# Seven products instead of eight in three more sets of a tile's up stage, and its attention steps at set slots

## The chip, the cores and the metric

The kernel runs on one core of one Trainium2 chip. The core has a matrix engine (PE, with its weight loader PEld), a vector engine (DVE), a scalar engine (ACT), a general engine (POOL) and a queue engine (SP) that only issues transfers; each works through its own instructions in order and waits on semaphores for the others. The metric is the device time of one execution in microseconds. Three runs of the kernel before took 1019.09, 1018.75 and 1016.43 us, so their median is 1018.75 us. The execution that was profiled took 1014.55 us.

## The reference

```python
# q, k, v: (8, 8, 576, 64), float32
scores = scale * np.matmul(q, k.transpose(0, 1, 3, 2))
gamma = 1.0 - 2.0 ** (-5.0 - np.arange(H, dtype=np.float32))
Dmat = np.where(rel >= 0, gamma[:, None, None] ** rel[None, :, :], 0.0)
ret = scores * Dmat[None, :, :, :]
attn_out = np.matmul(ret, v)
# (B, H, S, D) -> x: (4608, 512)
g = x @ w_gate                      # 512 -> 1536
silu = g * (1.0 / (1.0 + np.exp(-g)))
val = x @ w_val
return silu * val @ w_out           # 1536 -> 512
```

A retention attention without softmax gives 4608 tokens of 512 features; a gated feed-forward block follows. All is float32.

## The kernel before, in words

**Tiles and stages.** The tokens are worked in five tiles: tile 0 has 512 tokens, tiles 1 to 4 have 1024 each. What the change calls tile two is the second of them, `n == 1` in the code. Each of the big tiles has an up stage (`up_stage`, both projections and the gating) and a down stage (`down_step`, 26 steps, the output projection). The attention of the tokens that the next tile needs runs in between as attention steps (`tick`): there is one for each batch and pair of heads, and it is put between two pieces of the stages' work.

**The up stage.** The 1536 hidden columns are taken in three thirds (`qd` 0, 1, 2). For each third the product of the tile with the weights is made by a two-level scheme of the Strassen-Winograd kind. The outer level turns it into seven sets, worked in the order `SETS = (1, 2, 6, 7, 4, 5, 3)`. Each set is itself a product of two by two blocks, and is made either plainly, by eight products (`whole_slot`), or again by seven (`slot`). `PLAIN` lists the sets of tile two that are made plainly. One product is one slot: two matmuls of 128x128 weights with 128x256 activations, one for the gate and one for the value (`multiply`, L1186). A plain set is eight slots, filling four PSUM banks one after the other, two slots each; a seven-product set has five slots of its own (products 1, 5, 2, 6, 3) and leaves its products 7 and 4 to be put between the slots of the set that follows.

**Who reads the banks.** For a plain set, DVE adds each full bank to what the other sets left (`whole_read`, `combine` at L1042): one read for each of the four corners, two in set 5. For a seven-product set the bank is read while the sum in it grows: products 6, 7 and 4 are accumulated into the bank of product 1, product 3 into that of product 5, and each further product may be written only when the reading before it is done (`first_read`, `second_read`). That is seven reads for most sets. Corner results of sets 2, 4, 5 and 3 lie in four buffers (`ends`, one for each corner in tile two); `finish` takes them from there: ACT makes the SiLU (L1200) and DVE or POOL the product with the value part (L1201; in tile two DVE, but POOL for set 2 and in the last third). `clear` sees to it that a corner's buffer is finished before another set writes to it.

**Sums of operands.** The seven-product form needs sums of the blocks of the weights and of the tile. In tile two POOL makes the weights' sums during the stage itself (`w_outer`, `w_inner`, L1042), since SP also stores them for the later tiles (L1119 to L1122); they go through three block buffers in turn. The sums of a set of the tile's own blocks are made by `x_inner` (four sums of 128x256), and it overwrites one block of the set in place. The dictionary `after` holds at which slot each of these is issued; within an engine the order of issue is the order of work, and no engine waits for a slot as such.

**An attention step.** `tick` puts the matmuls of a step on PE at once and leaves the rest as pieces: ACT copies a state and the outputs to the next tile (L584, L656, L626), DVE masks the scores (L580, L590), makes the states (L596, L603, L608) and transposes the next queries and keys (L492, `qT` and `kT`); SP issues the loads of a later step (L282, L287). In the up stage a piece is taken at every second slot, and what is left is issued when the next step comes (`go_on(len(pieces))` at the head of `tick`). The scores of a step (L573) read the `kT` that the pieces of the step before it transposed.

**Where the steps stand.** In tile two's up stage of 157 slots, `merge` spreads six steps evenly over the slots from 56 on: they come ahead of slots 56, 73, 90, 106, 123 and 140, and the first of them has no matmuls. Four steps stand in the down stage, ahead of down steps 2, 7, 13 and 19:

```python
cut = (done + upto + (n == 1) * 2) // 2
merge((0.0, ticks(done, cut)), (0.5, ups))
for i, f in reversed(list(zip((2, 7, 13, 19), ticks(cut, upto), strict=True))):
    downs.insert(i, f)
```

The weights' operands of the down stage come through a ring of eight buffers (`fetch_one`), the first five over ACT's queue and the later ones over SP's.

Of the kernel before, what the change touches and what calls it, by code (L numbers as in the profile page):

```python
# [106 lines left out]


SETS = (1, 2, 6, 7, 4, 5, 3)
PLAIN = {(1, qd, o) for qd in range(3) for o in (1, 2, 4, 5, 3) if qd == 0 and o == 1 or o in (4, 5, 3)}  # L110


def terms(text):
# [18 lines left out]
def kernel(  # L132
# [45 lines left out]
    TW = 1024  # L178
    TB = TW // 4
    NF = DF // P  # L180
    NQ = NF // 4
# [32 lines left out]
    w_up = arena[:, QW : 4 * QW].rearrange("p (q g h k x) -> p q g h k x", q=NQ, g=2, h=4, k=2)  # L214
# [8 lines left out]
    xs = {0: rest[:, x0_at:dn_at].rearrange("p (h t) -> p h t", h=HP)}  # L223
    for n in range(1, NTILE):
        xs[n] = x_odd if n % 2 else rest[:, 0:QW].rearrange("p (h t) -> p h t", h=HP)
    at = [4096 + 512 * i for i in range(4)] + [x0_at + 512 * i for i in range(4)]
# [682 lines left out]
    for old, new in swaps.items():  # L909
        at = [i for i, line in enumerate(signed) if old in line]  # L910
# [136 lines left out]
    def x_sets(n):  # L1047

        x = xs[n].rearrange("p (K k) (T t x) -> p T K k t x", k=2, T=2, t=2)
        block = lambda a: rest[:, a : a + 1024].rearrange("p (k t x) -> p k t x", k=2, t=2)  # L1050
        sets = {1: x[:, 0, 0], 2: x[:, 0, 1], 4: x[:, 1, 1], 7: x[:, 1, 0], 5: block(4096), 6: block(5120), 3: block(x0_at)}
        spots = [rest[:, x0_at + 1024 + TB * i : x0_at + 1024 + TB * (i + 1)] for i in range(4)]
        spots += [rest[:, sum_at + 1024 + TB * i : sum_at + 1024 + TB * (i + 1)] for i in range(2)]
        spots += [rest[:, dn_at + 4096 + TB * i : dn_at + 4096 + TB * (i + 1)] for i in range(12)]
        spots += [operands[:, 5376 + TB * i : 5376 + TB * (i + 1)] for i in range(3)]
        new = {o: spots[3 * m : 3 * m + 3] for m, o in enumerate((4, 5, 1, 2, 6, 7, 3) if n == 1 else (1, 2, 7, 4, 5, 3, 6))}
        aside = new[3][2] if n > 1 else sets[1][:, 0, 1]

        def outer_sums(o, eng):
            a, b, sign = {5: (7, 4, 1), 6: (5, 1, -1), 7: (1, 7, -1), 3: (2, 6, -1)}[o]  # L1060
            return [lambda k=k: combine(eng, sets[o][:, k], sets[a][:, k], sets[b][:, k], sign) for k in range(2)]

        def inner_sums(o, eng):
            a, (s1, s2, s4) = sets[o], new[o]
            return [lambda: combine(eng, s1, a[:, 0, 1], a[:, 1, 1], 1),
                    lambda: combine(eng, s2, s1, a[:, 0, 0], -1),
                    lambda: combine(eng, aside if o == 1 else a[:, 0, 1], a[:, 0, 0], a[:, 0, 1], -1),
                    lambda: combine(eng, s4, a[:, 1, 0], s2, -1)]

        def put_back(eng):  # L1070
            a = sets[1]
            return [lambda: combine(eng, a[:, 0, 1], a[:, 0, 0], a[:, 0, 1], -1)]

        def view(o, i, qd):
            a, (s1, s2, s4) = sets[o], new[o]
            return {1: a[:, 0, 0], 2: a[:, 1, 0], 3: s4, 4: a[:, 1, 1], 5: s1, 6: s2, 7: aside if o == 1 and qd == 0 else a[:, 0, 1]}[i]

        return outer_sums, inner_sums, put_back, view, sets
# [55 lines left out]
    def up_stage(n):  # L1134

        busy, base = n == 1, used[0]
        x_outer, x_inner, put_back, x_at, x_raw = x_sets(n)
        seq = [(qd, o) for qd in range(NQ) for o in SETS]
        K = len(seq)
        plain = [(n, *e) in PLAIN for e in seq]  # L1140
        final = {2: (0, 0), 3: (0, 1), 4: (1, 0), 5: (1, 1)}
# [150 lines left out]
        slots, begins = [], []  # L1292
# [12 lines left out]
        if not busy:  # L1305
            begin = lambda k: begins[k]
            if n + 1 < NTILE:
                for i, f in enumerate(x_inner(2, nc.gpsimd)):
                    later(i, f)
                for i, f in enumerate(x_outer(7, nc.vector)):  # L1310
                    later(8 + 2 * i, f)
            for k, o in enumerate((6, 7, 4, 5, 3)):
                for i, f in enumerate(x_inner(o, nc.gpsimd)):
                    later(begin(k + 1) - (n + 1 == NTILE) * 3 + i, f)
            later(begin(6), *put_back(nc.gpsimd))
        else:
            for o, at in {7: 6, 1: 22}.items():
                for i, f in enumerate(x_inner(o, nc.gpsimd)):
                    later(at + i, f)
            for qd in range(NQ):  # L1320
                at = begins[len(SETS) * qd]
                _, _, w_outer, w_inner, store = w_sets(qd)
                if qd:
                    outers, inners = {5: 4, 6: 6, 7: 12, 4: 18}, {2: 0, 6: 8, 7: 14, 4: 20, 5: 27, 3: 34}
                else:
                    outers, inners = {7: 0, 4: 14}, {7: 2, 4: 18, 1: 28, 5: 35, 3: 39}
                for o, start in outers.items():
                    for i, f in enumerate(w_outer(o)):
                        later(at + start + i, f)
                for o, start in inners.items():  # L1330
                    for j, f in enumerate(w_inner(o)):
                        later(at + start + j, f)
                    later(at + start + 3, *store(o, True))
                if qd + 1 < NQ:
                    *_, next_inner, next_store = w_sets(qd + 1)
                    for j, f in enumerate(next_inner(1)):
                        later(at + (42 if qd else 44) + j, f)
                    later(at + (45 if qd else 47), *next_store(1, True))
                for i, o in enumerate((1, 2, 3, 5, 6, 7, 4)):
                    for j, f in enumerate(store(o, False)):  # L1340
                        later(at + (1, 2, 4, 8, 10, 15, 25)[i] + j, f)

        def go(at):
            for f in after.pop(at, ()):
                f()
            while waiting and waiting[0][0] <= at:
                finish(*waiting.pop(0)[1:])
            s = slots[at]
            (whole_slot if len(s) == 3 else slot)(*s, at)
            after_tick()  # L1350
            if at % (2 if busy or at >= 7 * len(SETS) else 3) == 1 and (busy or at % (7 * len(SETS)) < 36):
                part_on()
            if busy and at - begins[2 * len(SETS)] in (36, 38, 40):
                fetch_one()
            if at + 1 == len(slots):
                while waiting:
                    finish(*waiting.pop(0)[1:])
                for t in sorted(after):
                    for f in after[t]:
                        f()  # L1360
                after.clear()
                rested[:] = [i for b in free for i in range(4) if b is banks[i]]
                assert len(rested) == 4 and not taken
                if busy:
                    fetch_one()
                    fetch_one()
# [52 lines left out]
    def merge(*lists):  # L1419
        merged = [((i + d) / len(l), j, f) for j, (d, l) in enumerate(lists) for i, f in enumerate(l)]  # L1420
        for _, _, f in sorted(merged, key=lambda e: e[:2]):
            f()
# [81 lines left out]
    done = FIRST  # L1504
# [5 lines left out]
    ticks = lambda a, b: [lambda t=t: spread_tick(t) for t in range(a, b)]  # L1510
    for n in range(1, NTILE):
        upto = needed(n + 1) if n + 1 < NTILE else done
        cut = (done + upto + (n == 1) * 2) // 2
        ups = up_stage(n)
        if n == 1:

            for i in range(8 * len(SETS)):
                ups.pop(0)()
                if i in (13, 30):
                    wait = nc.sync.nop()  # L1520
                    tc.add_manual_dep(wait.ins, stepped[-1].ins.name,
                                      mybir.DependencyInfo(mybir.DependencyClass.Sync, mybir.DependencyReason.DATA), reason="loads in turn")
                    load(FIRST + i // 30)
        downs = [lambda i=i: down_step(n, i) for i in range(N)]
        if n == 1:
            merge((0.0, ticks(done, cut)), (0.5, ups))
        else:

            for i, f in reversed(list(zip((4, 52, 68, 102), ticks(done, cut)))):
                ups.insert(i, f)  # L1530
            merge((0.5, ups))
        if n == 1:

            for i, f in reversed(list(zip((2, 7, 13, 19), ticks(cut, upto), strict=True))):
                downs.insert(i, f)
            merge((0.5, downs))
        else:
            merge((0.0, ticks(cut, upto)), (0.5, downs))
        done = upto
# [30 lines left out]
```

## Time and profile before

| | |
|---|---|
| median of three runs | 1018.75 us (1016.43 to 1019.09) |
| profiled execution | 1014.55 us, its span 1012.8 us |
| PE busy | 1000.9 us, 99% of the span |
| DVE, POOL, ACT busy | 710.9, 561.8, 286.7 us |
| granted clock of PE | 1.000 |
| tile two's up stage | 172.2 to 319.4 us |
| tile two's down stage | 319.4 to 389 us |

The span runs from the first to the last instruction, and 1.75 us of the profiled execution lie around it. PE's matmul rows overlap their followers, so their busy time says little; the distance from one start to the next says how fast PE goes. A float32 matmul shows as two rows, so one slot is four rows. Rows of DVE, ACT and POOL that follow at once also overlap a little: two DVE reads in a row take less than twice one.

### The profile page before, as it was taken

The page shows a single profiled execution, that of the slowest core. Times are in us where ns is not written, and L with a number is a line of the kernel's source. Part 1 is how long each engine was busy: PE and PEld are TensorE (multiplying, and loading weights), DVE is VectorE, ACT ScalarE, POOL GpSimd, SP SyncE. Part 2 cuts the span into 40 slices and gives each one's busy share as a digit, 9 for nine tenths or more (in the row PEclk, how much of TensorE's full clock was granted, in tenths as well). Part 3 has the DMA queues.
Part 4 walks back from the last instruction along what each step waited for, and adds up shares of the span by engine and source line. Part 5 has one row for each costly group of instructions (what it writes and reads, how often), then busy time and mean ns, then how long its engine had stood idle before and what let it go on. Part 6 is the DMA issues. An engine that isn't in the chain of part 4 may idle for free.

```text
span 1012.8 us, 21319 instructions
## 1 busy us (share of the span) xinstructions
PE 1000.9 (99%) x8336; PEld 825.5 (82%) x8336; DVE 710.9 (70%) x1206; ACT 286.7 (28%) x636; POOL 561.8 (55%) x589
## 2 busy tenths in 40 slices
PE   6999999999999999999999999999999999999998
PEld 5655555888888888888888888888888888888887
DVE  4488887677875766977777678866575767566645
ACT  4565522132423312133422202233220012232110
POOL 3400359979375228575564157746672586566514
PEclk9999999999999999999999999999999999999999
DMA  9999866967587787647677777434454554445553
GB/s 245 261 288 272 192 216 234 264 193 214 138 238 207 217 231 193 198 156 196 184 202 206 198 179 217 154 133 159 161 172 141 154 189 147 148 155 180 182 159 102
DMA packets 278892, 194.38 MB, mean 192 GB/s; under 512 B 212552, under 2 KB 246088, under 8 KB 278792
## 3 DMA queue, kind: packets, MB, share of 16 engines
q1 hardware_dynamic: 251464, 94.70, 36.7%
q10 hardware_dynamic: 26688, 97.92, 29.1%
q8 instruction: 66, 1.08, 0.5%
q0 software_dynamic: 640, 0.39, 0.2%
q14 instruction: 34, 0.28, 0.1%
HBM read 154.04 MB, written 38.93 MB: 191 GB/s over the span
## 4 chain that ended last, share of the span: by engine, by line
PE 94%; DVE 2%; DMA 1%; POOL 1%; SPq 0%; issue 0%; ACT 0%; DVEq 0%; ACTq 0%; POOLq 0%
PE bankB L1186 12%; PE bankC L1186 11%; PE bankA L1186 11%; PE bankE L1186 11%; PE bankB L1392 7%; PE bankC L1392 7%; PE bankE L1392 6%; PE bankA L1392 6%; PE outer L532 2%; PE bankE L853 2%; PE bankA L853 2%; PE outer L1186 2%; PE inner L1186 2%; PE bankB L853 2%; PE outer L559 2%; PE bankC L853 2%
## 5 line engine op out<-in xcount | busy, mean ns | idle before, releaser
L1042 POOL TENSOR_TENSOR rest<-rest 128x512 f32<-128x512 f32 (+1 forms) x139 | 148.0, 1076 | 159.9 <-DVE rest L1042 112.5
L1201 POOL TENSOR_TENSOR arena<-rest,io 128x256 f32<-128x256 f32 x168 | 123.9, 750 | 89.4 <-ACT io L1200 88.9
L1200 ACT ACTIVATE io<-rest 128x256 f32<-128x256 f32 x192 | 79.3, 417 | 200.0 <-DVE rest L1042 140.0
L1186 PE MATMUL bankB<-rest,arena 128*128 128x256 f32 x448 | 114.5, 380 | 0.0
L1042 DVE TENSOR_TENSOR rest<-bankB,rest 128x512 f32<-128x512 f32 x116 | 78.5, 685 | 40.5 <-PE bankB L1186 28.5
L1186 PE MATMUL bankC<-rest,arena 128*128 128x256 f32 x416 | 106.3, 380 | 0.0
L1186 PE MATMUL bankA<-rest,arena 128*128 128x256 f32 x412 | 104.8, 379 | 0.0
L1042 DVE TENSOR_TENSOR rest<-bankA,rest 128x512 f32<-128x512 f32 x111 | 75.2, 685 | 40.8 <-PE bankA L1186 19.3
L1042 DVE TENSOR_TENSOR rest<-bankC,rest 128x512 f32<-128x512 f32 x110 | 74.5, 683 | 38.0 <-PE bankC L1186 23.4
L1042 DVE TENSOR_TENSOR rest<-bankE,rest 128x512 f32<-128x512 f32 x106 | 71.7, 684 | 36.2 <-PE bankE L1186 17.6
L1186 PE MATMUL bankE<-rest,arena 128*128 128x256 f32 x372 | 94.9, 380 | 0.3 <-DVE rest L1042 0.3
L1186 PEld LDWEIGHTS bankB<-rest,arena 128*128 128x128 f32 x448 | 84.7, 190 | 11.9 <-DVE rest L1042 0.2
L1186 PEld LDWEIGHTS bankC<-rest,arena 128*128 128x128 f32 x416 | 78.5, 190 | 11.4 <-DVE rest L1042 0.8
L1186 PEld LDWEIGHTS bankA<-rest,arena 128*128 128x128 f32 x412 | 78.1, 190 | 10.9 <-DVE rest L1042 0.2
L1186 PEld LDWEIGHTS bankE<-rest,arena 128*128 128x128 f32 x372 | 70.3, 190 | 10.4 <-DVE rest L1042 0.8
L1042 POOL TENSOR_TENSOR arena<-arena 128x256 f32<-128x256 f32 (+1 forms) x76 | 70.3, 947 | 11.1 <-PE bankC L1186 9.0
L886 POOL TENSOR_TENSOR rest<-rest 128x512 f32<-128x512 f32 x21 | 28.5, 1377 | 72.1 <-DVE rest L407 58.5
L1392 PE MATMUL bankB<-arena 128*128 128x256 f32 x264 | 61.0, 381 | 0.0
L1392 PE MATMUL bankE<-arena 128*128 128x256 f32 x264 | 60.8, 380 | 0.0
L1392 PEld LDWEIGHTS bankE<-arena 128*128 128x128 f32 x264 | 50.0, 190 | 6.9
L1392 PEld LDWEIGHTS bankB<-arena 128*128 128x128 f32 x264 | 49.8, 190 | 6.9
L1392 PE MATMUL bankC<-arena 128*128 128x256 f32 x240 | 55.2, 379 | 0.0
(270 smaller groups left out, 1876.0 us busy)
## 6 DMA issues: line engine op xcount, KB each, us to landing
arena<-up ACTq DMA_DIRECT2D x63, 896.0 KB, 4.6
arena<-dn ACTq DMA_DIRECT2D x65, 384.0 KB, 3.1
arena<-dn SPq DMA_DIRECT2D x39, 384.0 KB, 3.1
out_dram<-rest SPq DMA_DIRECT2D x31, 256.0 KB, 3.4
qk<-in_q_dram SPq DMA_DIRECT2D x108, 72.0 KB, 3.1
qk<-in_k_dram SPq DMA_DIRECT2D x108, 72.0 KB, 3.4
dn<-rest SPq DMA_DIRECT2D x26, 256.0 KB, 2.8
up<-arena SPq DMA_DIRECT2D x13, 512.0 KB, 5.6
```

Of the source, the lines that this page charges most:

```text
L532: m = nc.tensor.matmul(value(i, hl, c), s["v"][rows, at], ret[rows, c % 2 if whole(i) else hl, c // 2], start=start, stop=start, skip_grou ...
L559: nc.tensor.matmul(xr[half[hl]] if c + 1 == NC else value(i, hl, c), state[half[hl], c, :], s["qT"][half[hl], ts(c, L)], start=False, stop ...
L853: nc.tensor.matmul(bank, w, xs[0][:, c, :], start=(c == 0), stop=(c == HP - 1))
L886: eng.tensor_tensor(out=dst, in0=srcs[0], in1=srcs[1], op=ALU.add if op[0] == "add" else ALU.subtract)
L1042: eng.tensor_tensor(out=out, in0=a, in1=b, op=ALU.add if sign > 0 else ALU.subtract)
L1186: m = nc.tensor.matmul(b[:, g * TB : (g + 1) * TB], w[:, g], x, start=(opens and g == 0), stop=True, skip_group_check=True)
L1200: nc.scalar.activation(out=s, in_=src[:, 0:TB], func=AF.Silu)
L1201: (nc.vector if busy and o != 2 and qd + 1 < NQ else nc.gpsimd).tensor_tensor(out=hid[:, qd, 2 * H + h, 2 * T + t], in0=src[:, TB : 2 * TB ...
L1392: nc.tensor.matmul(b[:, m * TB : (m + 1) * TB], lhs[:, qd, ts(m, P)], w[:, qd], start=(opens and qd == 0 and m == 0), stop=(qd == NQ - 1), ...
```

## The change: three sets fewer in `PLAIN`, and slots given for the steps

Sets 3 of the second third and 4 and 3 of the last third are taken out of `PLAIN`, and so made by seven products. The stage has 154 slots instead of 157. `x_inner` is issued for set 3 from slot 38 of the second third and for set 4 from slot 17 of the last third, eight sums of 128x256 on POOL; their results go to room in the weights' region and in the next tile's. The steps of tile two's up stage stand ahead of slots 56, 70, 84, 97 and 111, one step fewer than before; the down stage has five, ahead of down steps 1, 5, 10, 14 and 19. Two of the first fetches for the down stage are issued one and three slots later.

```diff
-PLAIN = {(1, qd, o) for qd in range(3) for o in (1, 2, 4, 5, 3) if qd == 0 and o == 1 or o in (4, 5, 3)}
+PLAIN = {(1, qd, o) for qd in range(3) for o in (1, 2, 4, 5, 3) if qd == 0 and o == 1 or o in (4, 5, 3)} - {(1, 1, 3), (1, 2, 4), (1, 2, 3)}
...
+        if n == 1:
+            new[4] = [w_up[:, NQ - 1, 0, h, k, :] for h, k in ((0, 0), (1, 0), (0, 1))]
+            new[3] = [xs[2][:, h, TW - TB :] for h in range(3)]
...
-            for o, at in {7: 6, 1: 22}.items():
+            second, third = begins[len(SETS)], begins[2 * len(SETS)]
+            for o, at in {7: 6, 1: 22, 3: second + 38, 4: third + 17}.items():
...
-            if busy and at - begins[2 * len(SETS)] in (36, 38, 40):
+            if busy and at - begins[2 * len(SETS)] in (36, 39, 43):
                 fetch_one()
...
-        cut = (done + upto + (n == 1) * 2) // 2
+        cut = done + 5 if n == 1 else (done + upto) // 2
...
-            merge((0.0, ticks(done, cut)), (0.5, ups))
+            places_of = [i - 8 * len(SETS) for i in (56, 70, 84, 97, 111)]
         else:
-
-            for i, f in reversed(list(zip((4, 52, 68, 102), ticks(done, cut)))):
-                ups.insert(i, f)
-            merge((0.5, ups))
+            places_of = (4, 52, 68, 102)
+        for i, f in reversed(list(zip(places_of, ticks(done, cut)))):
+            ups.insert(i, f)
+        merge((0.5, ups))
...
-            for i, f in reversed(list(zip((2, 7, 13, 19), ticks(cut, upto), strict=True))):
+            for i, f in reversed(list(zip((1, 5, 10, 14, 19), ticks(cut, upto), strict=True))):
```

## The prediction, made before the changed kernel ran

> **What bounds the kernel now.** I read the page's busy times first, then the busy times by stretches, PE's waits in the stage, PE's order of time, and last the other engines' order of time where PE was nearest to waiting.
>
> ```profile
> PE 1000.9 (99%) x8336; PEld 825.5 (82%) x8336; DVE 710.9 (70%) x1206; ACT 286.7 (28%) x636; POOL 561.8 (55%) x589
> ...
> 172.35:319.60 147.25, 147.06 (x1242) 128.62 (x1241) 108.12 (x192) 44.16 (x107) 110.25 (x138) 1.00 0.72 202
> 319.60:389.00 69.40, 69.40 (x822) 60.88 (x821) 42.79 (x72) 19.30 (x55) 25.75 (x16) 1.00 0.79 215
> ...
> PE bankB L1186 <- ACT rest L1231: 0.2, 1, 0.2
> ```
>
> The two stretches are tile two's up and down stage; after the length come PE, PEld, DVE, ACT and POOL. PE is never without work, DVE and POOL are busy three quarters of the up stage, and PE's only wait there is 0.2 us. So fewer matmuls shorten the kernel as long as no new wait appears. How fast PE goes is read from starts:
>
> ```profile
> 180.82 1.03 PE L1186 MATMUL bankC<-x_odd,arena 128*128 128x256 f32 x4
> 181.69 1.03 PE L1186 MATMUL bankA<-rest,arena 128*128 128x256 f32 x4
> ...
> 251.38 0.46 PE L532 MATMUL outer<-ret,v 64*64 64x64 f32 x16
> ...
> 253.63 1.13 PE L1186 MATMUL bankB<-rest,arena 128*128 128x256 f32 x4
> 254.60 1.89 PE L1186 MATMUL bankA<-rest,arena 128*128 128x256 f32 x8
> ```
>
> One product (four rows) takes 0.863 us from start to start, not 1.03. An attention step takes 253.63 - 251.38 = 2.25 us, and the product behind it 0.10 more. The next rows are the stretch where PE came nearest to waiting, first DVE, then ACT, then POOL:
>
> ```profile
> 256.01 0.68 DVE L580 TENSOR_TENSOR ret<-inner,near 128x512 f32<-128x512 f32 x1
> 256.61 0.21 DVE L590 TENSOR_TENSOR ret_last<-outer,last_near 128x64 f32<-128x64 f32 x1
> 257.07 1.28 DVE L1042 TENSOR_TENSOR rest<-bankA,rest 128x512 f32<-128x512 f32 x2
> ...
> 266.69 0.77 DVE L492 STREAM_TRANSPOSE kT<-qk 128x576 f32<-128x576 f32 x1
> ...
> 272.82 0.21 ACT L656 COPY rest<-outer 128x64 f32<-128x64 f32 x1 [0.57 <-DVE ret_last L590]
> 272.93 1.13 ACT L626 COPY rest<-outer 128x256 f32<-128x256 f32 x3
> 274.09 0.59 ACT L1231 COPY rest<-bankB 128x512 f32<-128x512 f32 x1
> ...
> 251.88 4.33 POOL L1042 TENSOR_TENSOR arena<-arena 128x256 f32<-128x256 f32 x5
> 265.21 7.23 POOL L1042 TENSOR_TENSOR arena<-arena 128x512 f32<-128x512 f32 x7 [9.01 <-PE bankC L1186]
> 280.32 0.73 POOL L1201 TENSOR_TENSOR arena<-rest,io 128x256 f32<-128x256 f32 x1 [7.89 <-ACT io L1200]
> ```
>
> What to see: when a step comes, ACT's four output copies wait for `ret_last` on DVE and take 272.82 to 274.06, 1.24 us, and whatever ACT owes PE waits behind them (a bank copy; PE went on at 274.72, some 0.4 us late over two places). And POOL has two holes, 9.0 and 7.9 us.
>
> **What goes.** Three sets lose one product each: 3 x 0.863 = **-2.59 us**. The 0.4 us at 274 go too, as no step stands there any more: **-0.40**.
>
> **The moved step.** Its 136 matmul rows cost 2.35 us in either stage: 0. Its other work goes along: about 4.2 us of DVE, its ACT copies, and on SP ten to thirteen loads (5 to 6 us of issue). In the down stage DVE was busy 42.8 of 69.4 us and has room; steps there stand 4 or 5 down steps apart instead of 5 or 6. SP's operands of the down stage queue behind the loads, but eight buffers of 2.59 us each are 20 us of cover, against some 6. Price 0, up to 2 where one of DVE's sums is late (a rival). The loads themselves are issued up to 3 us nearer to their use in the up stage, with 13 us left: 0. The later fetches have over 10 us to their first use: 0.
>
> **The eight sums on POOL.** 8 x 0.69 = 5.5 us, in the holes of 9.0 and 7.9 us. Set 3's come right before the first hole and are done before PE needs them; set 4's come ahead of that set's weights' sums. Price on PE 0; without the holes each would cost its 0.7.
>
> **Nine reads more.** Seven reads a set instead of four, 0.60 us apart when they follow at once (257.07 and its pair take 1.28 with an end of 0.68): 5.4 us of DVE, while the step that left gives 4.2 back. On average that is hidden. It isn't at one place, which costs twice.
>
> Place one, `kT` of the step ahead of slot 97. The step before stands ahead of slot 84, 13 slots away (16 before), and the pieces are spread at the same pace, so that `kT` is transposed just ahead of the next step. DVE has in between, by the order of instructions: 9 reads (5.4), 5 products of `finish` (1.9), the step's own work (0.61 + 0.13 + 0.77 + 0.95 + 0.39 + two transposes of 0.69 = 4.2), it starts 0.45 late behind ACT's copy L584, and waits twice by some 0.6 at the start for a bank and a SiLU behind the four copies: 13.2 us. PE's 13 slots and the 1.6 us from the head of a step to its scores give 12.9. So 0.3 us late. The five products may be slower than that:
>
> ```profile
> L1201 DVE TENSOR_TENSOR arena<-rest,io 128x256 f32<-128x256 f32 x15 | 9.5, 636 | 1.6 <-ACT io L1200 1.6
> ...
> L1201 DVE TENSOR_TENSOR arena<-rest,io 128x256 f32<-128x256 f32 x5 | 2.1, 416 | 0.2 <-issue 0.2
> ```
>
> The first row is 197 to 253 us, with POOL busy, the second 256.3 to 265, in POOL's hole: 0.22 us each. With set 3's sums and the later clock POOL fills this place until about 261, so 5 x 0.22 = 1.1 us more. **+1.2 us** of bounds 0 and 2.4 (a DVE instruction or two more or less).
>
> [...]
>
> Place two, product 3 of the same set (slot 101). It accumulates into the bank of product 5, which DVE must have read; that read writes corner 22's buffer, which still holds the plain set's last corner, and so `clear` puts that corner's `finish` ahead of it. From the end of the step: product 1 full 0.98, read 0.60, `ret` 0.61, `ret_last` 0.21, ACT's four copies 0.05 + 1.24, the SiLU 0.42, DVE's product 0.05 + 0.41, the read 0.69 + 0.05: 5.3 us. PE is there after four slots, 3.45. **+1.9 us**, and 0.3 for a collision with POOL: **+2.2**, bounds 0 (ACT makes the SiLU ahead of the copies) and 3.2. Before, set 3 was plain and used corner 22 last.
>
> Smaller: the product after (slot 103) 0.25, and the last set of the stage, where 6, 3, 7 follow and product 7 waits for a read of 0.69 within one slot, 0.35: **+0.6**, bounds 0 and 1.5.
>
> Sum: -2.59 - 0.40 + 1.2 + 2.2 + 0.6 = **+1.0 us**, so 1014.55 + 1.0 = 1015.6 us for an execution like the profiled one. That execution lies 4.2 us below the median of the runs shown, so against the median it is 1018.75 + 1.0 = **1019.8 us**. Some 0.3%, 3 us, is what a measurement of this kernel can tell from no change: this is none.
>
> **The rivals**, all against the median. (A) The full gain: DVE and ACT keep up and PE doesn't wait. 1018.75 - 3.0 = 1015.8 us. For it: PE waited nowhere for DVE in this stage, with 108 us busy of 147. Against it: 14.8 of 16.2 us busy between 253.7 and 269.9, and steps that stand closer. (B) Slower: POOL is late for set 4's weights. Its sums wait for the hole's release by set 3 of the second third, at about 265, and for `finish` of set 2; from there four of those (2.8), outer sums (4.9), inner sums of set 7, x of set 4, weights of set 4 (8.3) take some 16 us, to about 295; PE needs the first at slot 132, about 298 with the waits above. It decides once POOL loses more than 4 us to collisions; then each further us is PE's. With POOL 30% slower, 2.5 us: 1018.75 + 1.0 + 2.5 = 1022.3. Against it: POOL's two holes. (C) The fifth step in the down stage makes a sum of DVE late; before, PE used one at 352.9 that ended at 352.6. One instruction of `reads` and one transpose ahead of it, with the hop itself: 1.5 to 2 us, 1021.5. [...] (E) The change doesn't do what it says: the order of instructions shows three products fewer and five steps, so no chance.
>
> **Numbers.** The forecast, gain and new waits nearly equal (1017 to 1021.8): 0.60. A 0.15, B 0.09, C 0.13, D 0.03. Below 1015.7 lies half of A: faster 0.08. Above 1021.8 lie most of B and D, a third of C and little of the forecast: slower 0.16. Within: 0.76. The range goes from A, with the scatter of three runs, 1015.2, to just beyond B, 1022.8.
>
> **What would show it.** Tile two's up stage 2.4 us shorter for the step that left, and otherwise 0 to 1 us longer; 12 matmul rows of L1186 fewer; a wait of PE at L573 for `kT`, and one of about 2 us at L1186 for a DVE read behind an L1201 whose release is ACT's SiLU. The down stage 2.4 us longer. If PE's waits show neither, it is A; if they name POOL's L1042, B; if they are at L1392, C.

## The result, and the profile after

The changed kernel took 1026.37 us (median of 1025.76, 1026.38, 1026.36 and 1029.57); the kernel before took 1018.25 us on the same chip. The ratio is 1.0095, with a 95% interval of 1.0074 to 1.0115: slower by almost one per cent, and outside the range of the prediction. The execution that was profiled took 1025.76 us, 11.2 us more than the profiled one of before.

The busy times of the page, as far as PE, show that the part meant to go did go: twelve matmul rows fewer than before (8336).

```profile
PE 1002.4 (98%) x8324; PEld 824.3 (81%) x8324; DVE 724.5 (71%) x1216; ACT 286.4 (28%) x636; POOL 567.3 (55%) x597
```

Next come the busy times by stretches, for the changed kernel. The stretches are tile two's up stage, its down stage as far as down step 22, and from there to tile three; after the length stand PE, PEld, DVE, ACT and POOL, then the granted clock.

```profile
173.02:318.85 145.83, 142.66 (x1093) 124.16 (x1092) 112.38 (x194) 40.28 (x97) 117.72 (x147) 1.00 0.75 209
318.85:388.12 69.27, 69.27 (x945) 60.72 (x944) 48.01 (x83) 23.14 (x65) 25.52 (x17) 1.00 0.68 172
388.12:406.87 18.75, 13.29 (x49) 10.96 (x48) 5.97 (x9) 0.00 (x0) 7.48 (x7) 0.82 0.82 236
```

From start to start, the same three took 147.26, 66.80 and 10.36 us before. So the up stage is 1.4 us shorter, the down stage up to step 22 is 2.5 us longer (the step that moved there), and the last four down steps are 8.4 us longer. With 0.8 us that were there at the stage's start, 0.8 in tile three and 0.1 behind it, that is the 11.2 us. PE's waits between 170 and 410 us name the place:

```profile
PE bankB L1396 <- DMA arena<-dn: 5.5, 1, 5.5
PE bankA L1189 <- DVE rest L1042: 2.9, 1, 2.9
PE outer L567 <- DVE kT L492: 0.2, 1, 0.2
```

The second and third are the two places that the prediction named. The first is not in it: down step 23 waits 5.5 us for its operand. PE's order of time there, first of the kernel before (down steps 22 and 23 and, after the mark, tile three's first product), then of the changed one (down steps 22 to 24, then the same):

```profile
386.26 2.75 PE L1392 MATMUL bankA<-arena 128*128 128x256 f32 x12
388.85 2.75 PE L1392 MATMUL bankE<-arena 128*128 128x256 f32 x12
...
396.62 1.03 PE L1186 MATMUL bankC<-rest,arena 128*128 128x256 f32 x4
```

```profile
388.12 2.75 PE L1396 MATMUL bankC<-arena 128*128 128x256 f32 x12
396.34 5.46 PE L1396 MATMUL bankB<-arena 128*128 128x256 f32 x12 [5.46 <-DMA arena<-dn]
401.59 2.86 PE L1396 MATMUL bankA<-arena 128*128 128x256 f32 x12
...
406.88 1.03 PE L1189 MATMUL bankE<-rest,arena 128*128 128x256 f32 x4
```

Two losses stand here, one behind the other. Step 23 comes 8.22 us after step 22 instead of 2.59, so 5.6 us late. And it then takes 5.25 us to the start of step 24 instead of 2.59 (2.7 more) although nothing is missing any more. Step 24 loses the last 0.1 us. The clock tells why; the granted clock is the number ahead of the last two:

```profile
390.00:394.00 4.00, 0.88 (x5) 0.42 (x3) 0.69 (x1) 0.00 (x0) 2.31 (x2) 1.00 0.41 82
394.00:396.00 2.00, 0.00 (x0) 0.00 (x0) 0.00 (x0) 0.00 (x0) 1.57 (x3) 0.74 0.92 334
396.00:402.00 6.00, 5.66 (x14) 4.59 (x15) 0.09 (x1) 0.00 (x0) 0.00 (x0) 0.52 1.04 256
```

From 395.0 to 401.8 us, 6.83 us, PE had half its clock; the kernel before shows no such stretch from its first record of the clock, at 17.2 us, to its end.

**Why the operand came late.** SP fetches it. Here are SP's transfers of the kernel before and then of the changed kernel (start, time from the first to the end of the last of the group, line, what):

```profile
372.58 1.06 SPq L290 DMA_DIRECT2D v<-in_v_dram  x2
...
374.32 0.89 SPq L997 DMA_DIRECT2D arena<-dn  x2
...
375.78 0.97 SPq L997 DMA_DIRECT2D arena<-dn  x2
389.24 0.39 SPq L1402 DMA_DIRECT2D out_dram<-rest  x1
```

```profile
382.24 9.16 SPq L290 DMA_DIRECT2D v<-in_v_dram  x2
391.44 0.55 SPq L293 DMA_DIRECT2D v<-in_v_dram  x1
392.09 0.41 SPq L997 DMA_DIRECT2D arena<-dn  x1
...
393.07 0.96 SPq L997 DMA_DIRECT2D arena<-dn  x2
```

Two loads of `v` took 1.06 us before and 9.16 us after: the second of them was issued only at 391.03, and behind it stand the operands of down steps 23, 24 and 25. The load needs nothing that is late: its buffer was free. In the trace SP's L290 waits 8.3 us for a transfer `arena<-up`, which ACT issued. What ties the two together is a completion semaphore. In the built program the transfers of SP and ACT share eight of these (`DMAHW0` to `DMAHW7`), in turn and in the order of the plan, and a load such as this one waits until the transfer eight before it, the last user of its semaphore, has landed. The listing of the changed program shows it (number in the plan, queue, transfer, and which transfer it waits for by its semaphore):

```
390  ACT  L999  arena<-up0_1   (tile three's first up operand; also waits for down step 21's matmuls)
...
397  SP   L290  v, first half  <- 389, SP, landed long ago
398  SP   L290  v, second half <- 390, the ACT fetch
399  SP   L293  v, last rows   <- 391
400  SP   L997  operand of down step 23
402  SP   L997  operand of down step 24
403  SP   L997  operand of down step 25
```

In the kernel before the same fetch is number 396, and its follower, 404, is the store of an output, behind all three operands. That is the 389.24 in the fence above: SP stood there longer still, from 376.75 on, 12.4 us of it in a wait for `arena<-up`, though the sum that it stores was ready at 377.8, but with nothing urgent behind it. The fetch itself waits on ACT for down step 21's matmuls to free its place, in both kernels; before, it was issued at 384.73, and SP's store went out 4.5 us later. The chain of work of the changed kernel, in this stretch, has the same links (start, length, what):

```profile
386.59 4.42 DMA arena<-up
...
391.03 0.37 SPq L290
...
392.09 4.12 DMA arena<-dn
...
396.34 5.46 PE bankB L1396 x12
```

Tile three's operand travels 4.42 us; 0.02 us after it has landed SP issues the held load of `v`, then the rest, and down step 23's operand can be used 4.25 us after its own issue (392.09 to 396.34).

**The two places in the up stage.** PE's product 3, then DVE's and POOL's rows of the changed kernel around it:

```profile
266.06 1.03 PE L1189 MATMUL bankB<-rest,arena 128*128 128x256 f32 x4
270.01 1.10 PE L1189 MATMUL bankA<-rest,arena 128*128 128x256 f32 x4 [2.93 <-DVE rest L1042]
```

```profile
265.73 0.22 DVE L590 TENSOR_TENSOR ret_last<-outer,last_near 128x64 f32<-128x64 f32 x1
267.58 1.49 DVE L1204 TENSOR_TENSOR arena<-rest,io 128x256 f32<-128x256 f32 x1 [1.63 <-ACT io L1203]
269.17 0.69 DVE L1042 TENSOR_TENSOR rest<-bankA,rest 128x512 f32<-128x512 f32 x1
```

```profile
266.30 2.48 POOL L1042 TENSOR_TENSOR arena<-arena 128x512 f32<-128x512 f32 x2 [2.58 <-PE bankC L1189]
```

The chain is the predicted one, link by link: the step's `ret_last`, ACT's four copies and SiLU (the 1.63 us of DVE's idle time), DVE's product, DVE's read, PE. Only the product took 1.49 us instead of 0.41, while two POOL sums ran beside it; it ended 0.3 us after them, and was 1.08 us longer beside 1.20 us of POOL's work. That these sums held it up is the author's reading of the two rows; no run shows it by itself.

### The profile page after: what moved, and what is told of

It is laid out like the page before. It is cut to its first block, busy times and chain, and to the rows that moved or that the text cites. A ratio compares the mean times of both kernels' runs of the same rounds, so it can differ in the third digit from the quotient of the medians.

```text
span 1024.0 us, 21333 instructions
## 1 busy us (share of the span) xinstructions
PE 1002.4 (98%) x8324; PEld 824.3 (81%) x8324; DVE 724.5 (71%) x1216; ACT 286.4 (28%) x636; POOL 567.3 (55%) x597
## 3 DMA queue, kind: packets, MB, share of 16 engines
q8 instruction: 66, 1.08, 0.5%
## 4 chain that ended last, share of the span: by engine, by line
PE 93%; DVE 2%; DMA 2%; issue 1%; POOL 1%; ACT 0%; SPq 0%; ACTq 0%; DVEq 0%; POOLq 0%
PE bankE L1189 11%; PE bankA L1189 11%; PE bankB L1189 11%; PE bankC L1189 11%; PE bankB L1396 7%; PE bankA L1396 7%; PE bankE L1396 7%; PE bankC L1396 6%; PE bankE L853 2%; PE bankA L853 2%; PE inner L1189 2%; PE outer L1189 2%; PE outer L532 2%; PE bankB L853 2%; PE bankC L853 2%; PE outer L559 1%
## 5 line engine op out<-in xcount | busy, mean ns | idle before, releaser
L1189 PE MATMUL bankA<-rest,arena 128*128 128x256 f32 x432 | 110.6, 380 | 3.2 <-DVE rest L1042 2.9
L1042 DVE TENSOR_TENSOR rest<-bankA,rest 128x512 f32<-128x512 f32 x122 | 82.5, 685 | 36.4 <-PE bankA L1189 18.9
L1189 PE MATMUL bankB<-rest,arena 128*128 128x256 f32 x404 | 103.7, 381 | 0.0
L1189 PE MATMUL bankE<-rest,arena 128*128 128x256 f32 x396 | 101.8, 381 | 0.0
L1189 PE MATMUL bankC<-rest,arena 128*128 128x256 f32 x392 | 100.2, 379 | 0.0
L1189 PEld LDWEIGHTS bankB<-rest,arena 128*128 128x128 f32 x404 | 76.1, 190 | 11.1 <-DVE rest L1042 0.8
L1189 PEld LDWEIGHTS bankE<-rest,arena 128*128 128x128 f32 x396 | 74.6, 190 | 11.4 <-DVE rest L1042 1.4
L1396 PE MATMUL bankA<-arena 128*128 128x256 f32 x264 | 61.1, 381 | 0.0
L1396 PEld LDWEIGHTS bankA<-arena 128*128 128x128 f32 x264 | 50.1, 191 | 7.0
L1396 PE MATMUL bankE<-arena 128*128 128x256 f32 x240 | 55.3, 380 | 0.0
```

The lines of the kernel that those rows point to most:

```text
L1042: eng.tensor_tensor(out=out, in0=a, in1=b, op=ALU.add if sign > 0 else ALU.subtract)
L1189: m = nc.tensor.matmul(b[:, g * TB : (g + 1) * TB], w[:, g], x, start=(opens and g == 0), stop=True, skip_group_check=True)
L1396: nc.tensor.matmul(b[:, m * TB : (m + 1) * TB], lhs[:, qd, ts(m, P)], w[:, qd], start=(opens and qd == 0 and m == 0), stop=(qd == NQ - 1), ...
```

## The experiments

Two theories of the 8.4 us were to be told apart. Mine: SP stops at a semaphore whose last user is a late fetch of ACT, which is a matter of where the steps' loads stand in the plan, and the half clock follows from PE's idleness. The rival: a fifth step's loads are simply too much for SP's queue ahead of the operands, or the products have a part in it. All stretches below are worked out from PE's starts in each profile, as those above were, and the half clock is that within them. They say more than the totals: tile two's up stage starts anywhere from 172.1 to 176.3 us in these profiles, a difference that arises ahead of everything that was changed.

| kernel | up stage | to down step 22 | to tile three | half clock, us |
|---|---|---|---|---|
| before | 147.26 | 66.80 | 10.36 | none |
| changed | 145.83 | 69.27 | 18.75 | 6.83 at 395.0 |
| x1_steps_only | 145.37 | 69.27 | 18.14 | 6.83 at 393.1 |
| x2_products_only | 150.84 | 66.80 | 10.36 | 3.41 at 265.9 |
| x3_one_later | 142.22 | 69.27 | 18.37 | 6.83 at 392.3 |
| x4_down_places | 146.29 | 69.86 | 10.36 | none |
| x5_both_places | 142.84 | 70.35 | 10.36 | none |
| x6_other_queue | 147.99 | 69.27 | 10.37 | 3.41 at 272.0 |
| x7_busy_wait | 148.47 | 69.27 | 16.29 | 3.41 at 273.5 |
| x8_own_room | 145.06 | 69.27 | 19.82 | 10.24 at 393.5 |
| x9_queue_and_slots | 143.02 | 69.27 | 10.38 | none |

### One half of the change alone: x1_steps_only and x2_products_only

The first has the places of the steps, and `PLAIN` as before:

```diff
-        cut = (done + upto + (n == 1) * 2) // 2
+        cut = done + 5 if n == 1 else (done + upto) // 2
...
-            merge((0.0, ticks(done, cut)), (0.5, ups))
+            places_of = [i - 8 * len(SETS) for i in (56, 70, 84, 97, 111)]
...
-            for i, f in reversed(list(zip((2, 7, 13, 19), ticks(cut, upto), strict=True))):
+            for i, f in reversed(list(zip((1, 5, 10, 14, 19), ticks(cut, upto), strict=True))):
```

> The products as before, only the attention steps at the set slots (five and five). Theory: the 5.5 us wait of down step 23 and the half clock after it come from where the fifth step's load stands among the transfers, not from the products; it is here in full, 5 us of wait and 2.6 us of half clock, and the kernel is 6 to 9 us slower than before. Rival (the products bring it, by the eight sums or by the earlier end of the up stage): no such wait, and no slower than before by more than 1 us.

The second has the three sets of seven products and the sums that belong to them, and the steps where they stood before:

```diff
-PLAIN = {(1, qd, o) for qd in range(3) for o in (1, 2, 4, 5, 3) if qd == 0 and o == 1 or o in (4, 5, 3)}
+PLAIN = {(1, qd, o) for qd in range(3) for o in (1, 2, 4, 5, 3) if qd == 0 and o == 1 or o in (4, 5, 3)} - {(1, 1, 3), (1, 2, 4), (1, 2, 3)}
...
+            places_of = [i - 8 * len(SETS) for i in (56, 73, 90, 106, 123, 140)]
```

> Seven products in the three sets, the steps as before (ahead of slots 56, 73, 90, 106, 123, 140 and of down steps 2, 7, 13, 19). Theory: no wait for an operand in the down stage and the full clock; in the up stage DVE is late for set 3 by 2 to 4 us, which eats the 2.6 us of the products, so 0 to 3 us slower than before. Rival (the products bring the down stage's wait): 5 us of wait at down step 23, 8 us or more slower.

Steps only: 1024.34 us, ratio 1.0078 (1.0061 to 1.0095). Products only: 1019.43 us, ratio 1.0036 (1.0024 to 1.0048). PE's waits in x1_steps_only:

```profile
PE bankE L1393 <- DMA arena<-dn: 5.5, 1, 5.5
PE outer L567 <- DVE kT L492: 0.9, 1, 0.9
```

and in x2_products_only:

```profile
PE bankB L1189 <- DVE rest L1042: 3.1, 2, 2.4
PE bankA L1189 <- DVE rest L1042: 0.5, 1, 0.5
PE bankE L1189 <- DVE rest L1042: 0.2, 1, 0.2
```

So the down stage's loss belongs to the steps and has nothing to do with the products, and the products by themselves don't pay either: with the steps at their old places, PE waits 3.8 us for DVE and runs 3.41 us at half clock, and the up stage is 3.6 us longer than before instead of 2.6 shorter.

### The steps at other places: x3_one_later and x4_down_places

```diff
-            places_of = [i - 8 * len(SETS) for i in (56, 70, 84, 97, 111)]
+            places_of = [i - 8 * len(SETS) for i in (56, 70, 84, 98, 112)]
```

> The changed kernel with the last two steps of the up stage one slot later, ahead of slots 98 and 112. Theory: the 3.3 us that PE waits at slot 101 come from ACT's four output copies, which the step puts ahead of the SiLU that corner 22 waits for; one slot later that SiLU is issued ahead of the step, and the wait shrinks to under 0.5 us: 2.5 to 3.5 us faster than the changed kernel. Rival (DVE has too much to do between slots 84 and 104, wherever the step stands): less than 1 us faster. The wait of down step 23 stays in both.

```diff
-            for i, f in reversed(list(zip((1, 5, 10, 14, 19), ticks(cut, upto), strict=True))):
+            for i, f in reversed(list(zip((1, 4, 8, 12, 18), ticks(cut, upto), strict=True))):
```

> The changed kernel with the down stage's steps ahead of down steps 1, 4, 8, 12 and 18. Theory: the load of the fourth step then stands before the transfer of the next tile's first operands in the count of the eight transfer semaphores, so SP doesn't stop ahead of the operands of steps 23 to 25: no wait over 1.5 us in the down stage, the clock stays full, 6 to 8.5 us faster than the changed kernel. Rival (five steps' loads are too much for SP's queue): a wait of 3 us or more for an operand stays, at step 23 or another.

x3_one_later took 1021.83 us, ratio 1.0055 (1.004 to 1.007); x4_down_places 1020.37 us, ratio 1.0038 (1.0023 to 1.0053). Each was measured beside runs of the kernel before, so against the changed kernel the ratios are compared: some 4 us less for the first, where 2.5 to 3.5 were expected, and some 6 for the second, where 6 to 8.5 were. One slot later, PE has no wait left in the up stage (142.22 us, 3.6 less than the changed kernel) and the one for the operand stays; with other places in the down stage, that wait goes with its half clock, and SP's loads of `v` pass. SP in x4_down_places:

```profile
381.61 1.96 SPq L290 DMA_DIRECT2D v<-in_v_dram  x2
...
384.76 1.38 SPq L997 DMA_DIRECT2D arena<-dn  x3
```

The same five steps and the same loads are issued in this stage, so their number isn't the cause. But the places also change what stands ahead of the operands, and so this run alone doesn't show that it is the semaphore.

### One transfer on another queue: x6_other_queue

In the built program POOL's transfers have completion semaphores of their own (`DMASW0` to `DMASW7`). So the one fetch that SP waited for was given to POOL, and the code is otherwise as the change left it. With the fetch out of the turn, each later transfer of SP and ACT gets the semaphore before its former one, and the second half of `v` follows a load of SP:

```diff
-        nc.scalar.dma_start(out=dst, in_=up_sets[a][SETS.index(i)])
+        queue = nc.gpsimd if fetched[0] == N + 1 else nc.scalar
+        queue.dma_start(out=dst, in_=up_sets[a][SETS.index(i)])
```

> The changed kernel with one transfer put elsewhere: the fetch of tile three's first up-stage operands (the first of L999's), issued by ACT so far, is issued by POOL, whose transfers have completion semaphores of their own. All slots of all steps, all waits for data and the order on SP stay. My theory (SP's load of v waited for this fetch because it was eighth after it in the turn of the semaphores that SP and ACT share, and the operands of down steps 23 to 25 stood behind it): SP no longer stops, PE has no wait at down step 23, no half clock follows; from down step 22 to the next tile 10.4 us instead of 18.8, and the time 7.5 to 8.5 us below the changed kernel, about 1018. Up stage as in the changed kernel, 145.8. Rival (SP's operands are late because the loads of a fifth step ahead of them take SP too long, by their number): the wait of 5.5 us stays, and the time within 1 us of the changed kernel. Second rival: the fetch itself lands late from POOL, and the wait comes at tile three's first product instead: 10.4 us becomes 12 or more, but with no wait at down step 23.

1019.98 us, ratio 1.0039 (1.0022 to 1.0056), where about 1018 us was expected. From down step 22 to tile three 10.37 us, as before the change. SP, the same instructions in the same order:

```profile
382.92 1.74 SPq L290 DMA_DIRECT2D v<-in_v_dram  x2
384.70 0.54 SPq L293 DMA_DIRECT2D v<-in_v_dram  x1
385.34 0.41 SPq L997 DMA_DIRECT2D arena<-dn  x1
...
386.33 0.97 SPq L997 DMA_DIRECT2D arena<-dn  x2
```

That settles it: with the shared semaphore out of the way, SP doesn't stop, although the fetch was issued later than ever (by POOL at 389.56). The rival falls. Down step 23's operand is issued 8.1 us ahead of its use (385.34 to 393.41), and as it takes some 4.25 us to be usable, about 4 us of slack were left; the prediction counted 20 us of cover against some 6.

The up stage wasn't the 145.8 us expected but 147.99. PE's product 3 waits 2.93 us, as in the changed kernel, and here a half clock follows:

```profile
271.07 1.18 PE L1190 MATMUL bankA<-rest,arena 128*128 128x256 f32 x4 [2.93 <-DVE rest L1043]
272.04 1.91 PE L1190 MATMUL bankE<-x_odd,arena 128*128 128x256 f32 x4
273.75 1.84 PE L1190 MATMUL bankB<-rest,arena 128*128 128x256 f32 x4
275.42 1.03 PE L1190 MATMUL bankC<-rest 128*128 128x256 f32 x4
```

Two products take 1.71 and 1.67 us instead of 0.863: 1.65 us lost. Why the same wait has this tail in one execution and not in another is taken up at the end.

### PE kept busy while it waits: x7_busy_wait

```diff
+        if n == 1 and i == 23:
+            for _ in range(11):
+                nc.tensor.matmul(outer[:, 1, 256:512], lhs[:, 0, 0:P], lhs[:, 0], start=False, stop=True, skip_group_check=True)
```

> The changed kernel with eleven more matmuls of 256 columns (2 x 0.216 us each, so 4.75 us together) ahead of down step 23's own. They go into a part of a bank that nothing reads and wait for nothing that is late; their work is extra and the result doesn't use it. PE is thereby busy during nearly all of its wait for the operands, which stay as late as they were. My theory (the half clock of 6.83 us comes from PE standing idle for 5.5 us, and not from the late operands or anything else at that time): the wait that is left is under 1 us, the granted clock stays at 1.00 through steps 23 to 25, down step 23 takes 2.7 instead of 5.25 us, and the time is 2 to 3 us below the changed kernel although it computes more. Rival (the clock dips there for another reason, or the fillers only lengthen the stage): the time is the same as the changed kernel's or above it, with clock 0.5 at 395 to 402 us.

1025.29 us, ratio 1.0075 (1.0053 to 1.0097). PE's order of time, where the extra matmuls are the first row and then come down steps 23 and 24:

```profile
395.49 4.91 PE L1396 MATMUL outer<-arena 128*128 128x256 f32 x22
401.34 2.83 PE L1399 MATMUL bankB<-arena 128*128 128x256 f32 x12 [0.94 <-DMA arena<-dn]
404.01 2.75 PE L1399 MATMUL bankA<-arena 128*128 128x256 f32 x12
```

Step 23 now takes 2.67 us at full clock, and the stretch is 2.46 us shorter than in the changed kernel, with 4.8 us of useless work in it: the half clock is the price of standing idle. The total was to fall by 2 to 3 us. By the two ratios to the kernel before, 1.0075 and 1.0095, it fell by some 2 us, but their intervals overlap, so the total doesn't show it; in this profile the up stage is 2.6 us longer than in the changed kernel's, with a half clock at 273.5 us behind the wait for product 3, as in x6_other_queue.

### A buffer of its own for the late corner: x8_own_room

```diff
+        def own_room(k, c):
+            return busy and (seq[k][1] == 4 and c == 21 or seq[k] == (1, 3) and c == 22)
...
-            if busy and o == 4 and c == 21:
+            if own_room(k, c):
...
-            for e in [e for e in waiting if o in final and e[1] != k and e[2] == c and number[seq[e[1]][1]] == number[o]]:
+            for e in [e for e in waiting if not (busy and seq[k] == (1, 3) and c == 22) and o in final and e[1] != k and e[2] == c and number[seq[e[1]][1]] == number[o]]:
```

> The changed kernel, in which corner 22 of the set with the late product 3 (slot 101 of tile two's up stage) gets a buffer of its own, so that DVE's read into it no longer has the last corner's finish ahead of it. My theory of that wait has two causes in a row: ACT's four output copies stand ahead of the SiLU, and DVE's product and read stand behind it. The buffer takes only the second away at slot 101; the finish is then done a little later and holds the next read. So the wait of 2.9 us at slot 101 goes, and one of 2 to 2.9 us comes up at slot 103: from the first up product to down step 0 145 to 146.3 us, as in the changed kernel (145.8), and the 5.5 us at down step 23 stay. Rival (the shared buffer alone is the cause): no wait over 0.5 us at slots 101 to 104, the stage 2.5 to 3 us shorter, about 143.

One execution: 1026.98 us. The wait at product 3 is gone, and two slots later there is this one:

```profile
269.16 1.03 PE L1192 MATMUL bankE<-x_odd,arena 128*128 128x256 f32 x4
272.35 1.13 PE L1192 MATMUL bankB<-rest,arena 128*128 128x256 f32 x4 [2.16 <-DVE rest L1042]
```

The shared buffer was where the lateness showed, not where it came from. It comes from the step that ACT and DVE have to work off in these slots; hence x3_one_later, which moves the step by one slot, removes it altogether. Down step 23 waits for its operand as before, here 6.3 us.

### The two cures together: x5_both_places and x9_queue_and_slots

```diff
-            places_of = [i - 8 * len(SETS) for i in (56, 70, 84, 97, 111)]
+            places_of = [i - 8 * len(SETS) for i in (56, 70, 84, 98, 112)]
...
-            for i, f in reversed(list(zip((1, 5, 10, 14, 19), ticks(cut, upto), strict=True))):
+            for i, f in reversed(list(zip((1, 4, 7, 11, 18), ticks(cut, upto), strict=True))):
```

> All of the change, with the five up-stage steps ahead of slots 56, 70, 84, 98 and 112 and the five down-stage steps ahead of down steps 1, 4, 7, 11 and 18. My theory: the two late places of DVE in the up stage (slots 97 and 101, 3.6 us together) go as they did in x3_one_later, and the wait of 5.5 us for down step 23's operands goes with its half clock as in x4_down_places, because the fetch of tile three's first operands now has its follower (eight transfers on) behind the operands of steps 23 to 25. From the first up product to down step 0 some 142.2 us, to down step 22 69.3 to 69.9, from there to the next tile 10.4: 222 us together, against 224.4 before and 233.9 in the changed kernel. The median 1.5 to 3 us below the kernel before, so at the edge of what can be told from no change. Rival: the two gains don't add, since another wait comes up once both are gone: then one of the three stretches is longer than said, and the time is that of the kernel before or above it.

x9_queue_and_slots has the up-stage places of this diff, the change's own down-stage places, and the edit of x6_other_queue.

> x6_other_queue with the up-stage steps at slots 98 and 112 as in x3_one_later; the down-stage steps stay where the change put them. By the stretches of those two runs: first up product to down step 0 142.2 to 142.8 us, to down step 22 69.3, from there to the next tile 10.4: 221.9 to 222.5 together against 224.4 before, so 2 to 2.5 us below the kernel before, 0.2%: the interval should lie below 1.000 or just reach it. Rival (the waits taken away leave nothing that five rounds can tell, as in x5_both_places): the stretches come out as said, and the ratio to the kernel before is within 0.998 to 1.002. Second rival: with the steps one slot later the fetch from POOL lands late, and a wait of PE for it shows at tile three's first product.

x5_both_places: 1017.70 us, ratio 0.9998 (0.9981 to 1.0014), so the expectation of 1.5 to 3 us was missed. Its three stretches come to 223.55 us, 0.9 less than before, not the some 2.4 expected. One of the missing microseconds is a stop in the middle of a down step for which the profile has no releaser:

```profile
354.09 1.78 PE L1396 MATMUL bankC<-arena 128*128 128x256 f32 x7
356.80 1.24 PE L1396 MATMUL bankC<-arena 128*128 128x256 f32 x5 [0.93 <-issue]
```

x9_queue_and_slots: 1015.06 us, ratio 0.9987 (0.9972 to 1.0002), three stretches of 222.67 us, 1.75 less than before, where 2 to 2.5 were expected. It is the fastest of all, but five rounds don't tell it from the kernel before. What is gained here is no more than the kernel's own scatter.

## Why the prediction was wrong

**Right.** The products: 12 rows fewer. The up stage was to be 1.3 us shorter by the sum (-2.59 - 0.40 + 4.0 of waits - 2.35 of the step); it is 1.4 shorter. The moved step costs the down stage 2.47 us (2.35). Both late places are where the prediction put them and wait for what it named (the row that waits for `kT` is L567, just ahead of the L573 that it gave). Of the sizes: `kT` ahead of slot 97 cost 0.4 us (the step took 260.71 to 263.36, 2.65 us, against 2.25) and not 1.2, since the products of `finish` there took 0.48 us each in the mean, not 0.64; product 3 cost 3.1 us (266.06 to 270.01, less 0.86) and not 2.2, since one product took 1.08 us more beside two POOL sums, where 0.3 was allowed; what is left of the stage's length, 0.4, was put at 0.6. Together 3.9 against 4.0: the errors cancel, so that the stage's sum came out is in part luck. One slip is in the sum itself: the two terms of place one, 0.3 and 1.1, make 1.4 and not 1.2. At down step 22 PE was 1.87 us later than before, of which 0.83 are from ahead of the stage: +1.04, where the sum says +1.0.

**Rivals.** A (no waits) and B (POOL late for set 4's weights) didn't happen; POOL is in none of PE's waits. D (0.03) is DVE's products held up by POOL's sums at place one: there they took 0.48 us each in the mean; at product 3 one took 1.49 us beside two such sums. C expected trouble in the down stage, but from DVE's sums; x1_steps_only shows the stage in trouble with DVE in time. By the prediction's own sign, a wait of PE in the down stage's matmuls, this would have been read as C; that a DMA ends the wait tells the two apart.

**The step that failed** is in the paragraph on the moved step: "SP's operands of the down stage queue behind the loads, but eight buffers of 2.59 us each are 20 us of cover, against some 6. Price 0". Two things are wrong in it. It counts what the loads take SP to issue, 5 to 6 us, but not what a load can wait for; the load of `v` stood 8.3 us (382.75 to 391.03) at a semaphore last used by another engine's transfer. And eight buffers are cover only if the queue gets to them as soon as they are free: x6_other_queue, where nothing stops SP, issues the operand 8.1 us ahead of its use, and before the change it was some 14 us (the second of the two at 374.32 in SP's fence, to 388.85). Price 5.6 us in place of 0. It could have been read ahead of the run: the order of transfers with their semaphores is in the built program, and the trace of before shows SP standing still from 376.75 to 389.24, right behind the operands of the last steps.

**The missing term.** The sum prices a wait by its length. Behind this one, PE ran at half clock through down step 23: 2.7 us more. x7_busy_wait, with 0.94 us of idle time there in place of 5.46 and the full clock behind it, shows that the idleness causes it. 5.6 and 2.7 us, with the 0.1 of step 24, are the 8.4 us by which the sum is off in this stage. The other 0.8 us, in tile three, have no cause that was shown: that tile's up stage took 139.4 to 141.0 us in these profiles without any change to it.

## What to carry to other kernels

When a step with transfers is moved, look not only at which buffers its transfers need, but at which completion semaphore each of them gets and who used it last: where queues share semaphores in turn, a transfer with nothing to wait for can stand behind a late one of another engine, and everything urgent behind it stands too (here a load for 8.3 us, and PE behind it for 5.5). One late transfer given to a queue with semaphores of its own can cure what otherwise takes new places for the work, chosen by that count (in x6_other_queue the last stretch went from 18.75 to 10.37 us). And a wait of the matrix engine of some two microseconds or more is to be priced with the half clock that may follow it (here 2.7 us behind a wait of 5.5 and 1.65 us behind one of 2.93), and with the chance that it doesn't: the same wait of 2.93 us at product 3 had one in x6_other_queue and x7_busy_wait and none in the changed kernel and x4_down_places.

## What the runs showed of the hardware

**The half clock went by fixed stretches of 3.41 us, and 2.01 us of idle time in one were enough.** All half-clock times above are multiples of 3.41 us (3.41, 6.83, 10.24). The starts of the clock's records in a trace lie whole multiples of 3.4133 us apart: 378.88, 6.83 and 621.23 us in the changed kernel (111, 2 and 182 of them), 996.69 us in the kernel before (292). If the span is divided into stretches of that length that begin where the half clock begins, PE's idle time in the stretch just ahead of it was 3.41 us (changed kernel, at 395.0), 2.81 (x1), 2.34 (x2), 3.26 (x3), 2.52 (x6), 2.93 (x7) and 2.01 (x8). The largest idle time in such a stretch of these profiles that was not followed by a half clock, from the first record of the clock on, is 1.77 us (x4, with the stretches reckoned back from the half clock at its end). x8_own_room also has 3.41 us of half clock long before tile two, at 24.8 us, behind a stretch with 1.82 us of idle time; the rest of that stretch was mostly attention matmuls of 64x64, so a sharp limit isn't shown. And the half clock stayed on after a stretch with 1.37 us (changed kernel) and 0.85 us (x8) of idle time and went after one with 0.50 (x2). By these figures the same wait of 2.93 us at product 3 has a tail in x6_other_queue and none in the changed kernel because in the changed kernel it lies across two stretches, with 1.59 and 1.33 us in them, while in x6_other_queue 2.52 us lie in one.
